# A decode step with cached keys: keys of one group per partition, and V's product from a zeroed tile with four diagonal blocks

## The chip, the core and the metric

The kernel runs on one core of one Trainium2 chip. The metric is the device time in microseconds (us) of one execution; the time of a version is the median over its runs. Engines are named as in the profile: PE (matrix products; PEld its weight loads), DVE (vector), ACT (scalar), POOL, and SP, which only issues DMAs here. The profile is of one execution, and its lines name a line of the kernel as L340.

## The reference

One token `x` (1024 values) goes through attention over a window of cached keys and, beside it, through an MLP; everything is added up.

```python
xn = layernorm(x)                                   # eps 1e-5, no gain
# attention: 32 query heads, 4 key/value heads ("groups"), 128 values a head, the last W = 4096 of 65536 keys
q = (xn @ wq).reshape(1, 1, 32, 128)                # wq 1024 x 4096
k = repeat(k_cache[:, :, -4096:, :], 8, axis=1)     # caches 1 x 4 x 65536 x 128
v = repeat(v_cache[:, :, -4096:, :], 8, axis=1)
p = softmax(q . k * 128 ** -0.5)                    # over the 4096 keys
a = (p . v).reshape(1, 1, 4096) @ wo                # wo 4096 x 1024
# MLP
y = layernorm(xn)
m = gelu_tanh(y @ w1 + b1) @ w2 + b2                # w1 1024 x 3584, w2 3584 x 1024
out = x + a + m
```

All inputs and the output are bfloat16. The weights and the windows of the caches are 39.9 MB, read once.

## The kernel before

**Plan.** The kernel lists its operations in one order by hand (`op`, `dma`), each with the names that it reads and writes. `Plan.emit` gives each engine its own operations in that order and adds a semaphore wait wherever an operation needs a result of another engine or of a DMA. An engine works its list strictly in order. A POOL operation that reads what the POOL operation before it wrote also waits for that one's semaphore.

**Loads.** Nearly all loads are issued by SP on one queue, in this order: one eighth of wq, K (four loads, one per group), the rest of wq (1, 2 and 4 MiB), b1, b2, w1 (two halves), V, w2 (three pieces), wo (two loads of 2 MiB, then five of 2, 1, 0.5, 0.25 and 0.25 MiB). They share four slots of 128 partitions x 32 KB: `slot[0]` holds K, then half of w1, then half of wo; `slot[1]` wq, w1, w2; `slot[2]` wq, V, the other half of wo; `slot[3]` the transposed scratch of K, then w2. A load into a slot waits until the slot's last reader is through; those behind it on SP wait with it.

**K and V in SBUF.** `load_k(g)` puts 32 rows of 32 KB (128 keys each) on the partitions g, g+4, g+8 and so on, so that four neighbouring partitions hold one row of each of the four groups. V is loaded with 32 keys of each group per partition, four pieces of 8 KB.

**Scores.** DVE transposes K in blocks of 32x32 (L340, four operations of 128x4096, into `slot[3]`), and ACT (18 copies, L345) and DVE (10 copies of 32x4096, L349) gather the blocks into `kT`, the keys with the head's 128 values over the partitions. The query goes through wq on PE into `acc2`, is copied to `q_sb` (L394, L395), turned by products with `selq` into `qo_ps`, and written as four blocks of 8 heads into the zeroed `qm` (L422). The score products (recorded at L233, tile `sc_ps`) take 4 column strips of 32 at a time, keys strided: the moving operand runs over (b, u, r) with every fourth key, the output likewise. `sc` is 128 x 1024: partition 32 R + head.

**Softmax.** `sc` is copied from PSUM (L433, L434); the maximum per partition (L441) is turned to a row (L443), joined over the four strips (L445, L447), turned back (L448), and ACT takes the exponential into `e128` with the row sums `l_loc` (L456). DVE transposes `e128` in 32x32 blocks into `eTb` (L460). The sums are joined through `sel4` (L462) to `rs`, one per head, and `grs` is `rs` under the mask `gmask` of a head's own group (L466).

**V's product.** `v_step` (L499 to L501) runs 32 steps, 30 of them in a PE loop of two per turn: weights `eTb[:, 32c : 32c+128]`, of which only the first 32 columns (32 heads) matter, moving operand the V of all four groups, 512 columns. So rows 0-31 of `qo_ps` hold each head against all four groups. DVE multiplies by `grs`, which leaves the own group (L517), adds over the groups (L519) and casts to `o_bf` (L521). Four products with `spread` bring it to 128 partitions (`o8_ps`), which ACT casts to `o8` (L544).

**MLP and the end.** w1's products run on PE in two parts: `w1_part(0)` behind the scores, `w1_part(1)` behind the maxima. `h_pre` (L470, DVE), Gelu (L472, ACT), the transpose `hT` (L474, DVE). Of w2's 28 rows, DVE adds 21 into `run[0]` and `run[1]` (L488 and L485), nine ahead of L517 and twelve behind L521 in its order; PE takes seven after V's product (`bulk_rows(PE_ROWS, ...)` into `sc_ps`), then wo's rows 0-23 into the same banks. L524 joins the two sums, L556 adds `sc_ps` to them, and PE, between wo's rows 27 and 28, adds that sum over the partitions by products with ones (L572, recorded at L239) into `acc2`. L575 (DVE) and L576 (ACT) copy the result, and SP and ACT store half of it each.

**POOL** writes the constants at the start (`spread` L260-261, `ident_f`, `selq`, `gmask` L272-275), computes two powers, zeroes `xw`, `qm`, `b1x` and `run[0]` (L327), and, once b2 has landed, adds x and b2 (L330) and places them in `run[0]` (L331); then it zeroes the last 96 columns of `eTb` (L459).

Of the kernel before, what the change touches and what calls it, by code (L numbers as in the profile page):

```python
# [7 lines left out]
FP32 = mybir.dt.float32  # L8
# [6 lines left out]
class Plan:  # L15
# [11 lines left out]
    def emit(self, done):  # L27
# [53 lines left out]
        ends.append(left)  # L81
        for n in done:
            value[n] = (nc.alloc_semaphore(f"dma{n}"), 16)
        for n, (eng, fn, r, w, dma, _) in enumerate(ops):
            if dma is not None:
                if n in done:
                    continue
                value[n] = (nc.alloc_semaphore(f"dma{n}") if dma is True else dma, 16)
                used.append(value[n][0])
            elif n in wanted:  # L90
                ticks[eng] += 1
                value[n] = (sems[eng], ticks[eng])
# [46 lines left out]
def kernel(  # L139
# [40 lines left out]
    def sb(name, shape, dt):  # L180
        return nc.alloc_sbuf_tensor(name, shape, dt).ap()
# [13 lines left out]
    k_sem = [nc.alloc_semaphore(f"k{g}") for g in range(Hkv)]  # L195
# [3 lines left out]
    def load_k(g):  # L199
        return nc.sync.dma_start(out=k_sb[g:P - Hkv + g + 1:Hkv, :],  # L200
                                 in_=A_k_cache[0, g, Sk - W:Sk, :].rearrange("(r c) d -> r (c d)", r=P // Hkv))
# [12 lines left out]
    def op(eng, fn, r=(), w=()):  # L214
        plan.add(eng, fn, r, w)
# [26 lines left out]
    for g in range(Hkv):  # L242
        plan.add("sp", lambda: None, (), (f"k{g}",), k_sem[g])
# [7 lines left out]
    for i, a, b in wq_cuts:  # L251
# [19 lines left out]
    gmask = sb("gmask", [Hq, Hkv], FP32)  # L271
    op("pool", lambda: pool.memset(gmask, 1.0), (), ("gmask",))  # L272
    op("pool", lambda: pool.affine_select(out=gmask, in_=gmask, compare_op=ALU.is_ge, fill=0.0, base=0,
                                          pattern=[[-REP, Hkv]], channel_multiplier=1), ("gmask",), ("gmask",))
    op("pool", lambda: pool.affine_select(out=gmask, in_=gmask, compare_op=ALU.is_ge, fill=0.0, base=REP - 1,
                                          pattern=[[REP, Hkv]], channel_multiplier=-1), ("gmask",), ("gmask",))

# [5 lines left out]
    for u in range(4):  # L283
# [33 lines left out]
       ("xn", "st12c", "st12g"), ("yT",))  # L317
    sel4 = sb("sel4", [P, Hq], FP32)
    op("dve", lambda: dve.tensor_reduce(out=sel4, in_=ident_f.rearrange("p (r h) -> p h r", r=4), axis=AX.X, op=ALU.add), ("ident_f",), ("sel4",))
    qm = sb("qm", [P, Hkv, Hq], BF16)  # L320
# [11 lines left out]
                                          compare_op=ALU.is_equal, fill=0.0, base=0, pattern=[[-1, Hq], [0, Hq]], channel_multiplier=1), ("xb32",), ("run0",))  # L332

# [5 lines left out]
    for s in range(NS):  # L339
        op("dve", lambda s=s: dve.transpose(out=scr[:, s, :], in_=k2[:, s, :]), ("k0", "k1", "k2", "k3", "slot0"), (f"scr{s}",))  # L340
# [38 lines left out]
    qz, zrow = qm.rearrange("p g h -> p (g h)")[0:Hq, :], spread.rearrange("p u n -> p (u n)")  # L379
# [19 lines left out]
    v4 = v_sb.rearrange("p (g c d) -> p g c d", g=Hkv, c=NCH)  # L399
    dma("sp", v_sb.rearrange("p (g n) -> p g n", g=Hkv), A_v_cache[0, :, Sk - W:Sk, :].rearrange("g (p c) d -> p g (c d)", p=P), (), ("v0",), ("slot2",))  # L400
# [19 lines left out]
    qm_d = qm.rearrange("p g h -> p (g h)")  # L420
    qm_d = bass.AP(tensor=qm_d.tensor, offset=qm_d.offset, ap=[list(qm_d.ap[0]), [Hq + REP, Hkv], [1, REP]])
    op("dve", lambda: dve.tensor_copy(out=qm_d, in_=qT_ps.rearrange("p k g -> p g k")), ("qo",), ("qm",))  # L422
    for g in range(Hkv):
# [34 lines left out]
    eTb = sb("eTb", [P, WQ4 + 96], BF16)  # L458
    op("pool", lambda: pool.memset(eTb[:, WQ4:], 0.0), (), ("eTb_pad",))  # L459
    op("dve", lambda: dve.transpose(out=eTb[:, :WQ4], in_=e128), ("e128",), ("eTb",))  # L460
# [35 lines left out]
    o_all = qo_ps[0:Hq, :]  # L496
    v_in = ("eTb", "eTb_pad", "v0", "slot2")

    def v_step(c, first, last):  # L499
        cols = eTb[:, bass.ds(32 * c, P)] if not isinstance(c, int) else eTb[:, 32 * c:32 * c + P]  # L500
        return pe.matmul(qo_ps, lhsT=cols, rhs=v4[:, :, c, :], start=first, stop=last)  # L501
# [78 lines left out]
    plan.emit([len(plan.ops) - 2, len(plan.ops) - 1])  # L580
# [30 lines left out]
```

## Time and profile before

| | before |
|---|---|
| median of 3 runs (lowest to highest) | 99.91 us (99.87 to 100.18) |
| the profiled execution: its own time | 99.88 us |
| its span from first to last instruction | 98.6 us |
| busy: PE, DVE, ACT, POOL | 59.4, 73.9, 30.8, 10.0 us |
| read from HBM | 39.86 MB, 404 GB/s over the span |
| V's product, start to end | 59.66 to 73.84 us |

The chain of waits is followed back from the last instruction; its pieces in order of time say what each moment of the span waited for. A timeline line gives start and length in us, engine, line, operation, out<-in with shapes, how many, and in brackets the idle time before it and what ended that. Several operations of one kind are merged to one line (x4), whose length then spans them. The rows of w1, w2, wo and the scores on PE all have the helper's line, L233 (weight loads L225, plain products L239), and are told apart by tile and shape.

### The profile page before, as it was taken

What the parts mean: (1) busy time and instruction counts of PE and PEld (TensorE: products, weight loads), DVE (VectorE), ACT (ScalarE), POOL (GpSimd) and SP (SyncE); (2) the same over time, 40 slices, a digit from 0 to 9 for tenths busy, and PEclk for the clock granted to TensorE, in tenths of its full rate; (3) what the DMA queues carried; (4) which work ended last, traced back from release to release, by engine and by line L of the source; (5) the groups of instructions that cost most, each with busy time, mean ns of one, the idle gap of its engine ahead of it and who ended that gap; (6) DMA issues with size and microseconds to landing.
All of it is one profiled execution on the core that took longest, in us unless ns stands there. A gap on an engine that the chain in (4) does not pass through costs nothing.

```text
span 98.6 us, 958 instructions
## 1 busy us (share of the span) xinstructions
PE 59.4 (60%) x323; PEld 16.6 (17%) x220; DVE 73.9 (75%) x75; ACT 30.8 (31%) x29; POOL 10.0 (10%) x22
## 2 busy tenths in 40 slices
PE   0032040599400699940899566887671899995792
PEld 0022000123000234400212111212211111111130
DVE  0023777999999999999103685999999999999231
ACT  0050000089999899992002095000000000000001
POOL 0072580000000670000000000000000000000000
PEclk9999999999998558995559999579998558999999
DMA  2999979999999899899799999999998999999970
GB/s 60 443 442 439 479 316 475 425 525 425 425 425 404 384 407 512 384 407 512 311 425 425 425 437 434 419 425 459 430 489 371 432 425 445 432 425 382 401 288 1
DMA packets 3133, 39.86 MB, mean 404 GB/s; under 512 B 439, under 2 KB 445, under 8 KB 829
## 3 DMA queue, kind: packets, MB, share of 16 engines
q1 hardware_dynamic: 3082, 39.86, 95.5%
q10 hardware_dynamic: 50, 0.00, 0.0%
q14 instruction: 1, 0.00, 0.0%
HBM read 39.86 MB, written 0.00 MB: 404 GB/s over the span
## 4 chain that ended last, share of the span: by engine, by line
DMA 64%; PE 25%; issue 4%; SPq 1%; DVE 0%
DMA slot<-in_A_wq_dram 27%; DMA slot<-in_A_wo_dram 20%; DMA slot<-in_A_v_cache_dram 17%; PE qo_ps L501 11%; PE acc L375 10%; PE acc L233 2%; PE acc L239 1%; SPq L219 1%; DVE res L575 0%
## 5 line engine op out<-in xcount | busy, mean ns | idle before, releaser
L345 ACT COPY kT<-slot 32x1024 bf16<-32x1024 bf16 (+1 forms) x18 | 23.9, 1327 | 14.2 <-DVE slot L340 14.0
L488 DVE SCALAR_TENSOR_TENSOR run<-slot,hTf,run 128x1024 f32<-128x1024 bf16 x20 | 24.2, 1270 | 0.0
L375 PE MATMUL acc<-slot,xw 128*128 x48 | 16.1, 514 | 11.6 <-DMA slot<-in_A_wq_dram 11.6
L340 DVE STREAM_TRANSPOSE slot<-slot 128x4096 bf16<-128x4096 bf16 x4 | 17.4, 4413 | 1.1 <-DMA slot<-in_A_k_cache_dram 1.1
L501 PE MATMUL qo_ps<-slot,eTb 128*128 (+1 forms) x32 | 11.3, 436 | 4.2 <-issue 2.9
L349 DVE COPY kT<-slot 32x4096 bf16<-32x4096 bf16 x10 | 13.2, 1316 | 0.2
L233 PE MATMUL sc_ps<-slot,o 128*1 128x512 bf16 x48 | 9.1, 379 | 1.6 <-DMA slot<-in_A_wo_dram 1.6
L375 PEld LDWEIGHTS acc<-slot,xw 128*128 x48 | 5.7, 118 | 22.7 <-issue 20.2
L576 ACT CAST res<-acc 33x224 bf16<-33x224 f32 x1 | 0.3, 339 | 20.4 <-PE acc L233 20.4
L233 PE MATMUL sc_ps<-slot,hT 128*1 128x512 bf16 x14 | 6.0, 618 | 0.5 <-DMA slot<-in_B_w_dram 0.5
L233 PE MATMUL sc_ps<-kT,qm 128*32 128x512 bf16 x32 | 5.7, 914 | 0.3 <-DVE qm L422 0.3
L501 PEld LDWEIGHTS qo_ps<-slot,eTb 128*128 (+1 forms) x32 | 3.1, 98 | 12.1 <-issue 8.7
L544 ACT CAST o<-misc 128x32 bf16<-128x32 f32 x1 | 0.2, 187 | 14.6 <-PE misc L239 14.6
L434 DVE COPY sc<-sc_ps 128x512 f32<-128x512 f32 x1 | 0.7, 692 | 5.3 <-PE sc_ps L233 5.3
L225 PEld LDWEIGHTS <-o 128*1 128x1 bf16 x40 | 2.4, 85 | 11.6 <-issue 10.9
L239 PE MATMUL misc<-x,spread 32*128 32x8 bf16 x4 | 0.3, 168 | 6.2 <-POOL spread L261 6.2
L239 PE MATMUL acc<-spread,qm 32*128 32x512 bf16 x4 | 1.6, 497 | 3.7 <-POOL qm L321 3.7
L255 DVE MEMSET mhalf<- 128x1 f32 x1 | 0.1, 59 | 5.0 <-PEq L209 5.0
L233 PE MATMUL acc<-slot,yT 128*1 128x448 bf16 x64 | 3.5, 353 | 0.0
L433 ACT COPY sc<-sc_ps 128x512 f32<-128x512 f32 x1 | 0.6, 591 | 8.4 <-PE sc_ps L233 8.4
L239 PE MATMUL qo_ps<-selq,q_sb 128*128 128x4 bf16 x8 | 0.4, 169 | 4.0 <-DVE q_sb L394 4.0
L257 ACT ACT_TABLE_LOAD x1 | 1.3, 1283 | 4.8 <-PEq L209 4.8
(88 smaller groups left out, 48.1 us busy)
## 6 DMA issues: line engine op xcount, KB each, us to landing
slot<-in_B_w_dram SPq DMA_DIRECT2D x3, 3584.0 KB, 16.6
slot<-in_A_wo_dram SPq DMA_DIRECT2D x3, 2048.0 KB, 23.2
slot<-in_A_k_cache_dram SPq DMA_DIRECT2D x4, 1024.0 KB, 9.6
slot<-in_A_wq_dram SPq DMA_DIRECT2D x1, 4096.0 KB, 26.9
slot<-in_A_v_cache_dram SPq DMA_DIRECT2D x1, 4096.0 KB, 16.5
slot<-in_A_wq_dram SPq DMA_DIRECT2D x2, 1024.0 KB, 9.1
slot<-in_A_wq_dram SPq DMA_DIRECT2D x1, 2048.0 KB, 17.7
slot<-in_B_w_dram SPq DMA_DIRECT2D x1, 2048.0 KB, 21.5
```

The source lines that it names most:

```text
L219: plan.add(eng, lambda: q.dma_start(out=out_ap, in_=in_ap), r, w, True, over)
L225: return pe.add_instruction(mybir.InstLdweights(name=nc.get_next_instruction_name(), engine=i.engine, tile_size=(P, 32), tile_position=pos ...
L233: return pe.add_instruction(mybir.InstMatmult(name=nc.get_next_instruction_name(), engine=i.engine, start_tensor_calc=start, stop_tensor_c ...
L239: op("pe", lambda: pe.matmul(out_ap, lhsT=w_ap, rhs=x_ap, start=start, stop=stop, tile_position=pos), r, w)
L257: op("act", lambda: act.activation(out=dummy[:, 0:1], in_=mhalf[0:1, 0:1], func=ACT.Exp), ("mhalf",), ("act_warm",))
L340: op("dve", lambda s=s: dve.transpose(out=scr[:, s, :], in_=k2[:, s, :]), ("k0", "k1", "k2", "k3", "slot0"), (f"scr{s}",))
L345: op("act", lambda s0=s0, s1=s1, R=R, Cd=Cd: act.copy(out=kT[32 * Cd:32 * Cd + 32, R, s0:s1, :].rearrange("p s (c j) -> p (s c) j", j=32), ...
L349: op("dve", lambda R=R, Cd=Cd: dve.tensor_copy(out=kT[32 * Cd:32 * Cd + 32, R, :, :].rearrange("p s (c j) -> p (s c) j", j=32), in_=T3[32 ...
L375: pe.matmul(acc2[:, b, :], lhsT=xw[:, bass.ds(32 * n + 512 * i, P)], rhs=slot[1 + i][:, bass.ds(1024 * n + 512 * b, 512)], start=False, st ...
L434: op("dve", lambda: dve.tensor_copy(out=sc[:, 0:512], in_=sc_ps[:, 0, :]), ("sc0",), ("scs0",))
L488: op("dve", lambda: dve.scalar_tensor_tensor(out=t, in0=wap, scalar=hTf[:, c:c + 1], in1=t, op0=ALU.mult, op1=ALU.add), (key, "hTf", f"run ...
L501: return pe.matmul(qo_ps, lhsT=cols, rhs=v4[:, :, c, :], start=first, stop=last)
```

## The change

- **Loads.** K is one load of 128 rows of 32 KB; partition 32 g + r holds keys 128 r to 128 r + 127 of group g. V is loaded in the same arrangement, 128 pieces of 32 KB instead of 512 of 8 KB.
- **Scores.** `kT[:, g]` now holds the keys of one group, so each of the four column strips works on one group g, and the four products that add up on a strip (u) are for the four blocks of 8 heads: `qm` has for each g and u a 32-column block that is zero outside columns 8u to 8u + 7. Row 32 g + 8 u + h of `sc` is head h of group g for the u-th quarter of the keys in each partition's 128. The moving operand reads runs of 32 neighbouring keys, and the output is written in order. As many weight loads and products as before. The maxima and sums are joined over u instead of over strips (`m_row`, `m_rep`, `sel4`), and `rs` is spread to 128 rows by `selr`.
- **Exponentials.** `eTb` holds after the transpose, for each partition 32 g + r, 128 keys x 8 heads. Four copies of 32 partitions (DVE, ACT, POOL, ACT) put these 8 columns at columns 8 g to 8 g + 7 of each 32-column block of `eM` (128 x 32 x 4 x 32), which POOL has zeroed.
- **V's product.** Step w takes four keys of every partition: weights `eM_w[:, 128 w : 128 w + 128]` (4 keys x 32 heads), moving operand the same four keys' V (4 x 128). Block u of the rows against block u of the columns is wanted: the four diagonal blocks of 32 x 128, which DVE, ACT, ACT and DVE copy into `o_u`, and which the products with `spread_f` (f32, 128 rows) add up while they spread the heads to 128 partitions. The division by the sum moves into ACT's copy to `o8` (`scale=rs`).
- **Gone**: `gmask` and its three POOL operations, `grs`, the zeroed tail of `eTb`, L517, L519, L521.
- **Output.** The two last copies count on one semaphore, so each of the two stores waits once instead of twice.

```diff
+        copied = nc.alloc_semaphore("copied")
+        ends.append(copied)
+        for n in last:
+            value[n] = (copied, len(last))
...
-    k_sem = [nc.alloc_semaphore(f"k{g}") for g in range(Hkv)]
+    k_sem = nc.alloc_semaphore("k")
...
-    def load_k(g):
-        return nc.sync.dma_start(out=k_sb[g:P - Hkv + g + 1:Hkv, :],
-                                 in_=A_k_cache[0, g, Sk - W:Sk, :].rearrange("(r c) d -> r (c d)", r=P // Hkv))
+    k_rows = A_k_cache[0, :, Sk - W:Sk, :].rearrange("g (r c) d -> g r (c d)", r=P // Hkv)
...
-    for i, sem in [(nc.sync.dma_start(out=slot[1][:, 0:NQ], in_=wq_v[:, 0, :]), wq_sem)] + [(load_k(g), k_sem[g]) for g in range(Hkv)] + [(nc.scalar.dma_start(out=x32, in_=x_flat.rearrange("(a j) -> a j", a=Hq)), x_sem)]:
+    for i, sem in [(nc.sync.dma_start(out=slot[1][:, 0:NQ], in_=wq_v[:, 0, :]), wq_sem)] + [(nc.sync.dma_start(out=k_sb, in_=k_rows), k_sem)] + [(nc.scalar.dma_start(out=x32, in_=x_flat.rearrange("(a j) -> a j", a=Hq)), x_sem)]:
...
+    selr = sb("selr", [P, P], FP32)
...
-    op("dve", lambda: dve.tensor_reduce(out=sel4, in_=ident_f.rearrange("p (r h) -> p h r", r=4), axis=AX.X, op=ALU.add), ("ident_f",), ("sel4",))
-    qm = sb("qm", [P, Hkv, Hq], BF16)
+    op("dve", lambda: dve.tensor_reduce(out=sel4.rearrange("p (g h) -> p g h", g=Hkv), in_=ident_f.rearrange("p (g u h) -> p g h u", g=Hkv, u=4),
+                                        axis=AX.X, op=ALU.add), ("ident_f",), ("sel4",))
+    op("dve", lambda: dve.tensor_copy(out=selr.rearrange("p (h q) -> p h q", q=4), in_=sel4.unsqueeze(2).to_broadcast([P, Hq, 4])), ("sel4",), ("selr",))
+    qm = sb("qm", [P, Hkv, 4, Hq], BF16)
...
+    eM = sb("eM", [P, NCH, 4, Hq], BF16)
+    op("pool", lambda: pool.memset(eM, 0.0), (), ("eM",))
+    spread_f = sb("spread_f", [P, 4, P], FP32)
+    op("pool", lambda: pool.memset(spread_f, 0.0), (), ("spread_f",))
+    for u in range(4):
+        op("pool", lambda u=u: pool.affine_select(out=spread_f, in_=spread_f, compare_op=ALU.not_equal, fill=1.0, base=P * u,
+                                                  pattern=[[-1, 4], [1, P]], channel_multiplier=-4), ("spread_f",), ("spread_f",))
...
-    v4 = v_sb.rearrange("p (g c d) -> p g c d", g=Hkv, c=NCH)
-    dma("sp", v_sb.rearrange("p (g n) -> p g n", g=Hkv), A_v_cache[0, :, Sk - W:Sk, :].rearrange("g (p c) d -> p g (c d)", p=P), (), ("v0",), ("slot2",))
+    dma("sp", v_sb, A_v_cache[0, :, Sk - W:Sk, :].rearrange("g (r c) d -> g r (c d)", r=P // Hkv), (), ("v0",), ("slot2",))
...
-    qm_d = qm.rearrange("p g h -> p (g h)")
-    qm_d = bass.AP(tensor=qm_d.tensor, offset=qm_d.offset, ap=[list(qm_d.ap[0]), [Hq + REP, Hkv], [1, REP]])
-    op("dve", lambda: dve.tensor_copy(out=qm_d, in_=qT_ps.rearrange("p k g -> p g k")), ("qo",), ("qm",))
-    for g in range(Hkv):
-        for R in range(4):
-            ldw(qm[:, g, :], (0, 32 * R), ("qm",))
+    qm_d = bass.AP(tensor=qm.tensor, offset=qm.offset, ap=[list(qm.ap[0]), [4 * Hq, Hkv], [Hq + REP, 4], [1, REP]])
+    op("dve", lambda: dve.tensor_copy(out=qm_d, in_=qT_ps.rearrange("p k g -> p g k").unsqueeze(2).to_broadcast([P, Hkv, 4, REP])), ("qo",), ("qm",))
+    for u in range(4):
+        for g in range(Hkv):
+            ldw(qm[:, g, u, :], (0, 32 * g), ("qm",))
...
-            for R in range(4):
-                kv = kT[:, R, :, :].rearrange("p u (b r h) -> p h b u r", r=8, h=Hkv)[:, g, 16 * a:16 * a + 16]
-                mm(sc_ps[32 * R:32 * R + 32, a, :].rearrange("p (b r u) -> p b u r", r=8, u=4), qm[:, g, :], kv,
-                   g == 0, g == Hkv - 1, (0, 32 * R), kt_keys, (f"sc{a}",))
+            for g in range(Hkv):
+                kv = kT[:, g, :, :].rearrange("p s (w u r) -> p u (s w) r", u=4, r=32)[:, u, 16 * a:16 * a + 16, :]
+                mm(sc_ps[32 * g:32 * g + 32, a, :].rearrange("p (w r) -> p w r", r=32), qm[:, g, u, :], kv,
+                   u == 0, u == 3, (0, 32 * g), kt_keys, (f"sc{a}",))
...
-    m_row = sb("m_row", [1, Hq], FP32)
-    op("dve", lambda: dve.tensor_reduce(out=m_row, in_=mT_ps.rearrange("a (r h) -> a h r", r=4), axis=AX.X, op=ALU.max), ("misc",), ("m_row",))
-    m_rep = sb("m_rep", [1, 4, Hq], FP32)
-    op("dve", lambda: dve.tensor_copy(out=m_rep, in_=m_row.unsqueeze(1).to_broadcast([1, 4, Hq])), ("m_row",), ("m_rep",))
+    m_row = sb("m_row", [1, Hkv, REP], FP32)
+    op("dve", lambda: dve.tensor_reduce(out=m_row, in_=mT_ps.rearrange("a (g u h) -> a g h u", g=Hkv, u=4), axis=AX.X, op=ALU.max), ("misc",), ("m_row",))
+    m_rep = sb("m_rep", [1, Hkv, 4, REP], FP32)
+    op("dve", lambda: dve.tensor_copy(out=m_rep, in_=m_row.unsqueeze(2).to_broadcast([1, Hkv, 4, REP])), ("m_row",), ("m_rep",))
...
-    mm32(mc_ps, m_rep.rearrange("a r h -> a (r h)"), ones_f[0:1, 0:1], True, True, ("m_rep", "ones_f"), ("misc",))
+    mm32(mc_ps, m_rep.rearrange("a g u h -> a (g u h)"), ones_f[0:1, 0:1], True, True, ("m_rep", "ones_f"), ("misc",))
...
-    eTb = sb("eTb", [P, WQ4 + 96], BF16)
-    op("pool", lambda: pool.memset(eTb[:, WQ4:], 0.0), (), ("eTb_pad",))
-    op("dve", lambda: dve.transpose(out=eTb[:, :WQ4], in_=e128), ("e128",), ("eTb",))
-    rs_ps = misc[0:Hq, 144:145]
-    mm32(rs_ps, sel4, l_loc, True, True, ("sel4", "l_loc"), ("misc",))
-    rs = sb("rs", [Hq, 1], FP32)
+    eTb = sb("eTb", [P, NCH * 4, REP], BF16)
+    op("dve", lambda: dve.transpose(out=eTb.rearrange("p c h -> p (c h)"), in_=e128), ("e128",), ("eTb",))
+    for g, e in enumerate(("dve", "act", "pool", "act")):
+        q = slice(32 * g, 32 * g + 32)
+        dst = eM[q, :, :, REP * g:REP * g + REP].rearrange("p w u h -> p (w u) h")
+        op(e, lambda e=e, q=q, dst=dst: act.copy(out=dst, in_=eTb[q]) if e == "act" else plan.engines[e].tensor_copy(out=dst, in_=eTb[q]), ("eTb", "eM", "spread_f"), (f"eM{g}",))
+    rs_ps = misc[:, 144:145]
+    mm32(rs_ps, selr, l_loc, True, True, ("selr", "l_loc"), ("misc",))
+    rs = sb("rs", [P, 1], FP32)
...
-    grs = sb("grs", [Hq, Hkv], FP32)
-    op("dve", lambda: dve.tensor_scalar_mul(out=grs, in0=gmask, scalar1=rs), ("gmask", "rs"), ("grs",))
...
-    o_all = qo_ps[0:Hq, :]
-    v_in = ("eTb", "eTb_pad", "v0", "slot2")
-    def v_step(c, first, last):
-        cols = eTb[:, bass.ds(32 * c, P)] if not isinstance(c, int) else eTb[:, 32 * c:32 * c + P]
-        return pe.matmul(qo_ps, lhsT=cols, rhs=v4[:, :, c, :], start=first, stop=last)
+    v_in = ("eM0", "eM1", "eM2", "eM3", "v0", "slot2")
+    eM_w = eM.rearrange("p w u h -> p (w u h)")
+    def v_step(w, first, last):
+        if isinstance(w, int):
+            cols, keys = eM_w[:, P * w:P * w + P], v_sb[:, 512 * w:512 * w + 512]
+        else:
+            cols, keys = eM_w[:, bass.ds(P * w, P)], v_sb[:, bass.ds(512 * w, 512)]
+        return pe.matmul(qo_ps, lhsT=cols, rhs=keys, start=first, stop=last)
...
-    o_m = sb("o_m", [Hq, Hkv, Dh], FP32)
-    op("dve", lambda: dve.tensor_tensor(out=o_m, in0=o_all.rearrange("h (g d) -> h g d", g=Hkv), in1=grs.unsqueeze(2).to_broadcast([Hq, Hkv, Dh]), op=ALU.mult), ("qo", "grs"), ("o_m",))
-    o_f = sb("o_f", [Hq, Dh], FP32)
-    op("dve", lambda: dve.tensor_reduce(out=o_f, in_=o_m.rearrange("h g d -> h d g"), axis=AX.X, op=ALU.add), ("o_m",), ("o_f",))
-    o_bf = sb("o_bf", [Hq, Dh], BF16)
-    op("dve", lambda: dve.tensor_copy(out=o_bf, in_=o_f), ("o_f",), ("o_bf",))
+    o_u = sb("o_u", [P, Dh], FP32)
+    for u, e in enumerate(("dve", "act", "act", "dve")):
+        blk = (slice(32 * u, 32 * u + 32), slice(Dh * u, Dh * u + Dh))
+        op(e, lambda e=e, blk=blk: (act.copy if e == "act" else dve.tensor_copy)(out=o_u[blk[0]], in_=qo_ps[blk]), ("qo",), (f"o_u{u}",))
...
-        mm32(o8_ps, spread[:, q, :], o_bf[:, 32 * q:32 * q + 32], q == 0, q == 3, ("spread", "o_bf"), ("misc",))
+        mm32(o8_ps, spread_f[:, q, :], o_u[:, 32 * q:32 * q + 32], q == 0, q == 3, ("spread_f", "o_u0", "o_u1", "o_u2", "o_u3"), ("misc",))
...
-    op("act", lambda: act.copy(out=o8, in_=o8_ps), ("misc",), ("o8",))
+    op("act", lambda: act.activation(out=o8, in_=o8_ps, func=ACT.Copy, scale=rs), ("misc", "rs"), ("o8",))
...
-    plan.emit([len(plan.ops) - 2, len(plan.ops) - 1])
+    end = len(plan.ops)
+    plan.emit([end - 2, end - 1], [end - 4, end - 3])
```

More of the change, by code (lines that the diff above doesn't have):

```diff
@@ L25, in add, with emit @@
         self.ops.append((eng, fn, tuple(r), tuple(w), dma, tuple(over)))
-    def emit(self, done):
+    def emit(self, done, last):
         nc, ops = self.nc, self.ops
@@ L89, in emit @@
                 used.append(value[n][0])
-            elif n in wanted:
+            elif n in wanted and n not in last:
                 ticks[eng] += 1
@@ L241 @@
     plan.add("sp", lambda: None, (), ("wq0",), wq_sem)
-    for g in range(Hkv):
-        plan.add("sp", lambda: None, (), (f"k{g}",), k_sem[g])
+    plan.add("sp", lambda: None, (), ("k",), k_sem)
     plan.add("act", lambda: None, (), ("x32",), x_sem)
@@ L270 @@
                                           pattern=[[32, 4]], channel_multiplier=1), ("selq",), ("selq",))
[L271 to L276, printed above, removed]
     ones_f = sb("ones_f", [P, P], FP32)
@@ L339 @@
     for s in range(NS):
-        op("dve", lambda s=s: dve.transpose(out=scr[:, s, :], in_=k2[:, s, :]), ("k0", "k1", "k2", "k3", "slot0"), (f"scr{s}",))
+        op("dve", lambda s=s: dve.transpose(out=scr[:, s, :], in_=k2[:, s, :]), ("k", "slot0"), (f"scr{s}",))
     pairs = [(R, Cd) for R in range(4) for Cd in range(4)]
@@ L377, in wq_rows @@
         return rows
-    qz, zrow = qm.rearrange("p g h -> p (g h)")[0:Hq, :], spread.rearrange("p u n -> p (u n)")
+    qz, zrow = qm[0:Hq, 0, :, :].rearrange("p u h -> p (u h)"), spread.rearrange("p u n -> p (u n)")
     for b in range(2):
@@ L419 @@
             mm32(qT_ps[:, k, :], blk, selq, True, True, (f"q_sb{b}", "selq"), ("qo",))
-    qm_d = qm.rearrange("p g h -> p (g h)")
-    qm_d = bass.AP(tensor=qm_d.tensor, offset=qm_d.offset, ap=[list(qm_d.ap[0]), [Hq + REP, Hkv], [1, REP]])
-    op("dve", lambda: dve.tensor_copy(out=qm_d, in_=qT_ps.rearrange("p k g -> p g k")), ("qo",), ("qm",))
-    for g in range(Hkv):
-        for R in range(4):
-            ldw(qm[:, g, :], (0, 32 * R), ("qm",))
+    qm_d = bass.AP(tensor=qm.tensor, offset=qm.offset, ap=[list(qm.ap[0]), [4 * Hq, Hkv], [Hq + REP, 4], [1, REP]])
[3 more added lines that the diff above has]
+            ldw(qm[:, g, u, :], (0, 32 * g), ("qm",))
         for a in range(2):
-            for R in range(4):
-                kv = kT[:, R, :, :].rearrange("p u (b r h) -> p h b u r", r=8, h=Hkv)[:, g, 16 * a:16 * a + 16]
-                mm(sc_ps[32 * R:32 * R + 32, a, :].rearrange("p (b r u) -> p b u r", r=8, u=4), qm[:, g, :], kv,
-                   g == 0, g == Hkv - 1, (0, 32 * R), kt_keys, (f"sc{a}",))
+            for g in range(Hkv):
+                kv = kT[:, g, :, :].rearrange("p s (w u r) -> p u (s w) r", u=4, r=32)[:, u, 16 * a:16 * a + 16, :]
+                mm(sc_ps[32 * g:32 * g + 32, a, :].rearrange("p (w r) -> p w r", r=32), qm[:, g, u, :], kv,
+                   u == 0, u == 3, (0, 32 * g), kt_keys, (f"sc{a}",))
     w1_part(0)
```

## The prediction

> **What bounds the kernel now.** I read the page's DMA rows first, then the chain of waits, then the timeline around each operation that the change touches.
>
> ```profile
> DMA  2999979999999899899799999999998999999970
> q1 hardware_dynamic: 3082, 39.86, 95.5%
> DMA 64%; PE 25%; issue 4%; SPq 1%; DVE 0%
> ```
>
> One queue is busy from the second slice to the last but one, 95.5% of the span: 39.86 MB. Compute is free as long as it never starves that queue and is done when the last rows of wo land. The chain of waits shows what follows them.
>
> ```profile
> 5.62 26.91 DMA slot<-in_A_wq_dram
> ...
> 43.02 16.51 DMA slot<-in_A_v_cache_dram
> ...
> 74.24 19.55 DMA slot<-in_A_wo_dram
> ...
> 93.83 1.03 PE acc L233 x16
> 94.87 0.86 PE acc L239 x8
> 95.73 0.66 PE acc L233 x12
> 96.39 0.02 issue
> 96.41 0.30 PE acc L233 x2
> ```
>
> From 93.8 us on PE is never free: wo rows 24-27, then the sum of `run` and `bulk` (L239), then rows 28-31. L239 needs L556, the last DVE work. So DVE has little room at the end. How much, these timeline rows say:
>
> ```profile
> 47.66 5.69 PE L233 MATMUL sc_ps<-kT,qm 128*32 128x512 bf16 x32 [0.29 <-DVE qm L422]
> 53.09 1.77 PE L233 MATMUL acc<-slot,yT 128*1 128x448 bf16 x32
> 58.14 1.25 DVE L460 STREAM_TRANSPOSE eTb<-e 128x1024 bf16<-128x1024 bf16 x1 [0.20 <-ACT e L456]
> 59.66 1.01 PE L501 MATMUL qo_ps<-slot,eTb 128*128 128x512 bf16 x3 [1.28 <-DMA slot<-in_A_v_cache_dram]
> ...
> 90.22 1.23 DVE L524 TENSOR_TENSOR run<-run 128x1024 f32<-128x1024 f32 x1
> ...
> 91.34 1.89 PE L233 MATMUL sc_ps<-slot,o 128*1 128x512 bf16 x16 [1.27 <-DMA slot<-in_A_wo_dram]
> 93.27 1.28 DVE L556 TENSOR_TENSOR run<-sc_ps,run 33x512 f32<-33x512 f32 x2 [1.82 <-PE sc_ps L233]
> ```
>
> L556 waited 1.82 us for PE, and PE 1.27 us for wo. V's product starts 0.1 us after V lands (59.53), with the exponentials ready at 59.39.
>
> **Loads.** V: 4 MiB landed at 59.53 in 8 KB pieces, the load ahead of it (w1's second half, issued 32.9, 16.6 to landing) at 49.55, so 9.98 us. The 4 MiB of wq in 32 KB pieces landed at 32.53, the load ahead (issued 5.1, 17.7 to landing) at 22.8: 9.73. V in 32 KB pieces therefore gains about 0.25 us. K's pieces are 32 KB before and after: 0. [...] Three of four K issues vanish (4 take 2.45 us), so all engines start some 1.8 us earlier; this gains nothing, as the transposes wait for K (15.45) and the queue is full. One wait fewer before the output: up to 0.05.
>
> **What POOL gets.** gmask's three operations go (0.45 us, early, hidden). New are a memset of `eM` (128x4096), one of `spread_f` (128x512) and four selects on it. They stand behind L331, which waits for b2 landing at 32.7, so they start at 35.2, inside DVE's ten kT copies (32.9 to 46.2). What happens there:
>
> ```profile
> 33.08 2.19 POOL L331 TENSOR_SCALAR_AFFINE_SELECT run<-xb 32x1024 f32<-32x1024 f32 x1
> 35.23 1.24 POOL L459 MEMSET eTb<- 128x96 bf16 x1
> ...
> 34.17 2.19 DVE L349 COPY kT<-slot 32x4096 bf16<-32x4096 bf16 x1
> 36.37 1.22 DVE L349 COPY kT<-slot 32x4096 bf16<-32x4096 bf16 x1
> ...
> 12.59 1.82 DVE L316 TENSOR_SCALAR yT<-xn,st 128x8 bf16<-128x8 f32 x1 [0.67 <-POOL st L314]
> 12.64 0.84 POOL L326 MEMSET b1x<- 128x896 bf16 x1
> 13.43 0.95 POOL L327 MEMSET run<- 128x1024 f32 x1
> ```
>
> These rows exclude each other. L331 stood until the first copy ended (34.15), then worked 1.0 us, and the second copy took 2.19 instead of 1.22. L459's 96 columns took 1.24, until that copy ended. A 128x8 operation (yT) took 1.82 us and ended 0.03 after the memset of `run`. So a POOL memset delays a DVE copy by its own length. Lengths: memsets of 1024 and 128 columns took 0.95 and 0.19, 0.85 ns a column, the same in bf16 (0.84 for 896); 4096 columns make 3.55, 512 make 0.51. The nearest row to the selects is L261, of the same pattern on 32 partitions, 0.64: four are 2.55. Sum 6.6; I take 6.5, since the start of a DVE operation hides about 0.1. kT is then done at 52.7. Bounds: 0, if POOL were held back until DVE is through, and 7.1 (memset at 0.95 for each 1024, selects at 0.7).
>
> **Scores.** qm is written 128 columns wide instead of 32: +0.1 (L422 0.19). The score products now read runs of 32 keys and write in order. They went in fours, eight in turn: 0.85 apart at clock 0.50, 0.46 at full clock. w1's products (448 contiguous columns, full clock) went 0.22 per four (1.77/8). So contiguous costs half: 8 x 0.43 = 3.4 at half clock, which PE has again after its idle stretch, instead of 5.7, less what the full clock gave the last four. I take -2.1; bounds 0 (the layout isn't the cause) and -3.7 (full clock).
>
> **Ahead of V's product.** Four copies of 32x1024 from `eTb` into `eM`. ACT has two, 1.04 each (L345, same shape), behind its table load and warm-up, which end 0.2 after the transpose: 2.3 in all. DVE: 0.35 to 1.1; POOL: 1.0 (L331's work) to 2.2. ACT ends last; PE's first product waits for all four, later by 2.1. Gelu is queued behind them on ACT. Sum: 6.5 + 0.1 - 2.1 + 2.1 = 6.6, so V's product runs from 66.3 to 80.5 (14.2 before: same 32 steps of 128 x 512). That is soon enough for wo's second half, queued behind loads that land until 86.4; past about 83 the queue would run dry.
>
> **Side path.** h_pre follows the eM copy on DVE (65.5), Gelu the ACT copies (67.1), hT 68.8; the first nine w2 rows on DVE run 69 to 79.3 instead of 63.64 to 74, still ahead of V's end.
>
> **After V.** L517, L519 and L521 took 73.85 to 75.77; two copies of 32x128 on DVE (0.2 each, as L521) and two on ACT take 0.5. DVE gains 1.4. Its last twelve rows are queued behind its two copies: 81.0 to 95.4, L524 to 96.6, L556 to 97.9 (94.55 before). The room was 1.82 + 1.4, and 0.2 between L556 and L239: 6.6 - 3.5 = 3.1. PE: the f32 product with `spread_f` costs 0.5 per piece (L239's f32 weights, two loads 0.50), 2.0 instead of 0.28; w2's rows start at 83.1, and with 3.0 at full clock, 7.2 for wo's first 16 rows and 1.9 for the next eight, PE is done at 95.2, ahead of DVE. scale=rs on o8 is free (rs long ready). selr, sel4, m_row, m_rep: under 0.3, hidden or even.
>
> **Sum.** The profiled execution took 99.88 (span 98.6 and 1.28 around it), 0.03 under the median of three, 99.91. 99.88 + 3.1 = **103.0**. V's 0.25 and the wait of 0.05 don't show, since DVE's sum, no longer the landing, ends the kernel.
>
> **Rivals.**
> - *PE at half clock in w2's rows.* Before, the clock was 0.50 from 75.5 to 82.3 and the seven rows took 5.96 instead of 3.0. For: V's end is again followed by weight loads and waits; against: the pause is 0.5 instead of 2 us. PE then ends `bulk` at 98.2, and the end is 4.7 later: 104.6.
> - *Less exclusion.* Only the memset of `eM` holds DVE (3.5): V starts 3.6 late, 0.1 beyond the room, and a slower copy adds some: 100.3. For: selects wait on each other, and could fall into DVE's gaps; against: L331 is such a select, and delayed a copy by all its work.
> - *The loads stay the bound (not slower).* If POOL yields and its work falls between or after DVE's copies, V's product starts at most 0.1 late, under the room of 3.5; below a delay of 3.5 the end is set by wo's landing, earlier by V's 0.25: 99.6. For: POOL did wait for copies one and two. Against: copy two waited as well.
> - *Rows 16 MiB apart.* K's and V's rows of four groups, 16 MiB apart (65536 keys of 256 B), are now read at the same time. If that halved the rate, K alone adds 9.7: 109 or more. Against: wq's rows, 64 KB apart, and V before, whose pieces also come from four groups, went at full rate. [...]
>
> **Numbers.** Chances: forecast 0.45, half clock 0.25, less exclusion 0.13, loads stay the bound 0.13, far rows 0.04. The measurement tells 0.3% (0.3 us) from no change. Slower: 0.45 + 0.25 + 0.04 + most of 0.13 = 0.85; faster and same share the fourth case, at their border: 0.06 and 0.09, with a little of the third. The forecast's own range is 101.6 (scores gain 3.7) to 104.2; the range goes down to the fourth case, 99.6, and up to 105.0 for the half clock.
>
> **What would show it.** In the profile after: kT copies ending near 52.7, one of them over 4 us; score products of some 3.5 us; L501 starting near 66, released by an eM copy rather than V; DVE without a pause before L556, and L239 waiting for it; V landing 9.7 us after the load ahead. If the kT copies end near 46, the forecast is wrong; if PE enters w2's rows at 0.50 and DVE waits at L556, the first rival holds.

## The result and the profile after

The changed kernel took 257.02 us (median of six runs, 254.94 to 260.0) beside 99.89 for the kernel before on the same chip (99.79 to 100.18): a ratio of 2.562, 95% interval 2.553 to 2.570. The forecast was 103.0, its range ended at 105.0. The profiled execution took 260.0, 1.2% above the median: 256.6 of span and 3.4 around it, where before had 98.6 and 1.28. Two of the six runs, the profiled one among them, were in a slower state at 260 and are left out of the ratio; the other four had spans of 251.7 to 254.2, so 2 to 5 us of what follows belong to that state. The sum that has to be explained in the profile is 158.0 us inside the span and 2.1 outside it.

From the page of after, the DMA row of the timeline, the row of the loading queue, the chain by engine, and the group of K's transposes (in a group: busy time, mean ns of one, then idle time before it and what ended it):

```profile
DMA  7999993222222221998299999999982222227910
q1 hardware_dynamic: 2626, 39.86, 62.5%
another core or an unknown queue 62%; DVE 17%; PE 8%; DMA 8%; issue 2%; POOL 1%; ACT 0%; SPq 0%; POOLq 0%; DVEq 0%
L344 DVE STREAM_TRANSPOSE slot<-slot 128x4096 bf16<-128x4096 bf16 x4 | 17.4, 4413 | 79.0 <-DMA slot<-in_A_k_cache_dram 79.0
```

The bytes are the same 39.86 MB, but two long stretches show a DMA share of two tenths. The chain gives 62% of the span to a queue that it can't name; the group's row names it: VectorE stood 79.0 us before the first transpose, for K. The chain of waits, in order of time (start, length, what), shows both places:

```profile
13.28 78.96 another core or an unknown queue
92.26 17.43 DVE slot L344 x4
...
110.97 5.65 DVE kT L353
...
138.18 79.57 another core or an unknown queue
```

K is complete at 92.26 instead of 15.45, V at 217.8 instead of 59.53. From V's landing to the end of the span before took 39.1 us (98.6 - 59.5), and after takes 38.8 (256.6 - 217.8). So the whole loss lies ahead of V's landing: 76.8 in K, and 81.4 between K and V. Everything that the prediction computed for the engines is covered by these two waits, and had to be looked for in other kernels.

Two facts of the trace say what K's load does. A load's semaphore shows an update for each of its landings. K's received four (82.7, 83.2, 91.3 and 92.2 us, after one update at the issue), V's also four (209.5 to 217.8), while in the kernel before each load of K, V and the weights received 16. And a 32 KB piece took about 2.5 us (median) while K was under way, instead of 1.213. K is 128 pieces, over four engines 32 each. They ran from 4.95 to 92.2 us, so 2.7 us each on the engine that ended last: 2.5 or 3.8 while other engines moved wq, until about 41 us, and 2.3 in the mean from 45 to 80. Over sixteen engines at 1.213 it would be 9.7 in all. The loss has two factors, four from the number of engines and a little over two from the duration of a piece.

### The profile page after: what moved, and what is told of

Read it like the earlier page. It is cut to its first block, busy times and chain, and to the rows that moved or that the text cites. A ratio compares the mean times of both kernels' runs of the same rounds, so it can differ in the third digit from the quotient of the medians.

```text
span 256.6 us, 975 instructions
## 1 busy us (share of the span) xinstructions
PE 56.4 (22%) x327; PEld 16.9 (7%) x224; DVE 78.8 (31%) x75; ACT 33.4 (13%) x33; POOL 20.6 (8%) x25
## 3 DMA queue, kind: packets, MB, share of 16 engines
q1 hardware_dynamic: 2626, 39.86, 62.5%
HBM read 39.86 MB, written 0.00 MB: 155 GB/s over the span
## 4 chain that ended last, share of the span: by engine, by line
another core or an unknown queue 62%; DVE 17%; PE 8%; DMA 8%; issue 2%; POOL 1%; ACT 0%; SPq 0%; POOLq 0%; DVEq 0%
DMA slot<-in_A_wo_dram 8%; DVE kT L353 7%; DVE slot L344 7%; PE qo_ps L506 4%; PE acc L235 1%; PE sc_ps L235 1%; PE misc L241 1%; DVE yT L310 1%; DVE m_loc L443 0%; DVE xn L299 0%; PE acc L241 0%; DVE q_sb L398 0%; POOL spread L262 0%; ACT sc L435 0%
## 5 line engine op out<-in xcount | busy, mean ns | idle before, releaser
L506 PE MATMUL qo_ps<-slot,eM 128*128 (+1 forms) x32 | 11.1, 436 | 82.8 <-DMA slot<-in_A_v_cache_dram 79.7
L353 DVE COPY kT<-slot 32x4096 bf16<-32x4096 bf16 x10 | 18.3, 1831 | 0.2
L379 PEld LDWEIGHTS acc<-slot,xw 128*128 x48 | 5.6, 116 | 101.4 <-issue 99.0
L506 PEld LDWEIGHTS qo_ps<-slot,eM 128*128 (+1 forms) x32 | 3.1, 98 | 90.5 <-issue 88.5
L327 POOL TENSOR_TENSOR xb<-x,b 32x32 f32<-32x32 bf16 x1 | 0.2, 233 | 96.7 <-DMA b<-in_B_b_dram 96.7
L335 POOL TENSOR_SCALAR_AFFINE_SELECT spread_f<-spread_f 128x512 f32<-128x512 f32 x4 | 5.7, 1427 | 0.6
L235 PE MATMUL sc_ps<-slot,hT 128*1 128x512 bf16 x14 | 4.9, 524 | 0.9 <-DMA slot<-in_B_w_dram 0.9
L331 POOL MEMSET eM<- 128x4096 bf16 x1 | 3.5, 3501 | 0.0
L235 PE MATMUL sc_ps<-kT,qm 128*32 128x512 bf16 x32 | 3.3, 586 | 0.4 <-DVE qm L424 0.4
L465 POOL COPY eM<-eTb 32x1024 bf16<-32x1024 bf16 x1 | 1.3, 1282 | 15.7 <-DVE eTb L461 15.7
L235 PE MATMUL acc<-slot,o 128*1 128x288 bf16 (+1 forms) x32 | 2.2, 272 | 0.6 <-DMA slot<-in_A_wo_dram 0.6
L310 DVE TENSOR_SCALAR yT<-xn,st 128x8 bf16<-128x8 f32 x1 | 2.1, 2136 | 0.7 <-POOL st L308 0.7
```

Source lines behind the costliest of these rows:

```text
L235: return pe.add_instruction(mybir.InstMatmult(name=nc.get_next_instruction_name(), engine=i.engine, start_tensor_calc=start, stop_tensor_c ...
L310: op("dve", lambda: dve.tensor_scalar(out=yT, in0=xn, scalar1=st12[:, 2:3], scalar2=st12[:, 6:7], op0=ALU.subtract, op1=ALU.mult), ("xn", ...
L331: op("pool", lambda: pool.memset(eM, 0.0), (), ("eM",))
L335: op("pool", lambda u=u: pool.affine_select(out=spread_f, in_=spread_f, compare_op=ALU.not_equal, fill=1.0, base=P * u, pattern=[[-1, 4], ...
L353: op("dve", lambda R=R, Cd=Cd: dve.tensor_copy(out=kT[32 * Cd:32 * Cd + 32, R, :, :].rearrange("p s (c j) -> p (s c) j", j=32), in_=T3[32 ...
L379: pe.matmul(acc2[:, b, :], lhsT=xw[:, bass.ds(32 * n + 512 * i, P)], rhs=slot[1 + i][:, bass.ds(1024 * n + 512 * b, 512)], start=False, st ...
```

## Experiments on the loads

The table view by windows gives both factors at once: the window and its length, busy time (and instructions) of PE, PEld, DVE, ACT and POOL, granted clock, DMA share and GB/s. A share of 0.25 is four of sixteen engines, as K's four landings. Before, in the stretch in which K loads:

```profile
6.00:15.00 9.00, 2.47 (x10) 1.31 (x10) 4.91 (x17) 0.24 (x2) 5.14 (x14) 1.00 0.99 425
```

After, while K alone loads:

```profile
45.00:80.00 35.00, 0.00 (x0) 0.00 (x0) 0.00 (x0) 0.00 (x0) 0.00 (x0) 1.00 0.25 56
```

Per busy engine that is 425 / (0.99 x 16) = 27 GB/s before and 56 / (0.25 x 16) = 14 after. What differs is the access pattern: K's source in one load runs over [4 groups, 32 rows, 4096], groups 16 MiB apart, while each of the four loads before ran over 32 rows. The landings fit the outermost dimension of the source in the loads here: 4 gives four, 128 and 32 give sixteen, and loads of 16 rows (below) kept all engines busy (a DMA share of 0.97). Even the trace of before has a case of four: b1's load, four rows, landed four times (32.2 to 32.3). Which rule deals the pieces to engines beyond these cases is not shown.

The half rate was the open question. The theories were the distance of the rows in memory (rival 4) and the partitions that the engines write. The code below is cut from longer lines ("..."), and in the versions with several loads each operation that uses K or V waits for all of them.

**Four loads each, same arrangement.** Groups stay on 32 neighbouring partitions (V in the same way):

```
-... (nc.sync.dma_start(out=k_sb, in_=k_rows), k_sem) ...
+... (nc.sync.dma_start(out=k_sb[32 * g:32 * g + 32, :], in_=k_rows[g]), k_sem[g]) for g in range(Hkv) ...
```

> The changed kernel with K and V loaded in four loads each, one per group (32 rows of 32 KB onto 32 neighbouring partitions); all else as changed. Theory A (a load whose outermost dimension is the 4 groups is carried by 4 of the 16 DMA engines; everything else behaves about as forecast): each load again counts on 16 engines, K lands near 15.5 us, and the time is 101.3, worked out with the sizes that the changed kernel's own trace shows (kT copies 5.1 longer, scores 2.4 shorter). Rival B (the arrangement itself, one group on 32 neighbouring partitions, loads slowly however it is split): over 150. If nothing of the compute matters: 99.6.

Measured: 122.93 (122.57 to 123.17), ratio 1.230 (1.228 to 1.232). Sixteen landings a load, yet 1 MiB came every 4.9 to 5.0 us (landings 11.1, 16.2, 21.2, 26.1) instead of 2.43, a piece at 2.55 (median). The window over K's load:

```profile
7.00:26.00 19.00, 1.62 (x4) 0.63 (x4) 4.93 (x15) 0.00 (x0) 4.24 (x6) 1.00 0.96 203
```

All engines busy, half the bytes: 203 / (0.96 x 16) = 13 GB/s per engine. The four engines were most of the loss (257 to 123), but the arrangement itself halves the rate, although at any time all engines read one group, so no rows 16 MiB apart.

**K alone in one load** (V as in the experiment above).

> V in four loads as in e1_four_loads, K in one load as in the change. This prices K's load alone. Theory A: half of the loss, 170 to 185; K's semaphore gets 4 landings from DMA engines, K's 32 KB pieces take some 2.5 us as in the changed kernel (1.21 before), and the last lands 80 to 92 us after the start. Rival B: the same as e1_four_loads.

Measured: 203.3 (one run), above the 170 to 185 expected; the last of four landings at 92.2, pieces of 2.44 us (median) and 55 GB/s in the window from 45 to 80 us. So one load instead of four costs 80 us for K (203.3 - 122.9), and for V, on top of K's, about another 54 (257.0 - 203.3).

**K in one load, its four blocks near each other.** The blocks come from one group, 33 rows (1.03 MiB) apart instead of 16 MiB (V in four loads):

```
+k_all = A_k_cache[0, 0, 0:132 * 128, :].rearrange("(b r c) d -> b r (c d)", b=4, c=128)
+k_rows = k_all[:, 0:32, :]
```

> As e2_k_one_load, but K's four blocks of 1 MiB are read from 1.03 MiB (33 rows of 32 KB) apart inside one group instead of 16 MiB apart; so the scores are of other keys. Still 4 DMA engines. Theory HBM (the pieces take twice as long because four engines read 16 MiB apart): 32 KB pieces at 1.21 us, K there by about 45 us, time 125 to 140. Theory port (they take twice as long because of where the four engines write): pieces at 2.5 as before, 170 to 185.

Measured: 203.48 (one run), pieces of 2.41 (median), 58 GB/s in the same window. The distance changes nothing here, so it isn't what halves the rate. It could still have cost something that the other limit hides; the next experiment answers that.

**Still four engines, still 16 MiB apart, but other partitions.** Each of four loads takes eight rows of every group onto 32 neighbouring partitions, so the four engines write partitions 8 apart instead of 32 (V in four loads):

```
+... (nc.sync.dma_start(out=k_sb[32 * g:32 * g + 32, :], in_=k_rows[:, 8 * g:8 * g + 8, :]), k_sem[g]) for g in range(Hkv) ...
```

> As e2_k_one_load, but K in four loads, each of 8 rows from each of the four groups onto 32 neighbouring partitions; still 4 DMA engines and still 16 MiB apart, but the four engines now write partitions 8 apart instead of 32 apart. Keys stand on other partitions than the kernel takes them for. Theory port: 32 KB pieces at 1.21 us, K there by about 45 us, time 125 to 140. Theory HBM: pieces at 2.5, 170 to 185.

Measured: 169.71 (one run). Four landings a load, the last of them at 23.3, 42.6, 52.2 and 61.9. While the other engines still loaded, pieces took 2.3 to 2.55, so K was complete at 61.9 and not near the 45 expected; from 42 us on, with four engines alone, 1.213:

```profile
42.00:60.00 18.00, 0.00 (x0) 0.00 (x0) 0.00 (x0) 0.00 (x0) 0.00 (x0) 1.00 0.24 106
```

The same share of 0.24, at 106 instead of 56 GB/s, 28 per engine. Number of engines and distance of the groups are as in the change, only the partitions differ: the doubling comes from where the engines write, and with rows 16 MiB apart four engines reach the full rate, so rival 4's mechanism falls. Side by side, per busy engine: 14 GB/s with four engines 32 partitions apart (after), 13 with sixteen engines on 32 neighbouring partitions (four loads), 28 with four engines 8 apart, and 27 with sixteen engines on every fourth partition (before). Why some sets of partitions take half the rate is not shown.

**Can the arrangement be loaded at full rate?** My guess was that it could, if partitions 0 to 63 (groups 0 and 1) and 64 to 127 (groups 2 and 3) were written at the same time. At the rate of before K would then be complete near 15.5 us, at that of the four loads near 26. Three tries. Eight loads of 16 rows, groups in turn 0, 2, 0, 2, 1, 3, 1, 3:

```
+turns = [(g + d, h) for g in (0, 1) for h in (0, 1) for d in (0, 2)]
+... (nc.sync.dma_start(out=k_sb[32 * g + h:32 * g + 31 + h:2, :], in_=k_rows[g][h:32:2]), k_sem[i]) for i, (g, h) in enumerate(turns) ...
```

> The changed kernel with K and V in eight loads each: 16 rows of one group onto every second of its 32 partitions, the loads alternating between the groups of partitions 0-63 and those of 64-127 (0, 2, 0, 2, 1, 3, 1, 3); each load on 16 engines, one 32 KB piece each. [...]

Measured: 119.47 (ratio 1.195, 1.192 to 1.198), 0.5 MiB every 2.35 to 2.4 us, K landed at 25.0: still half rate, with 221 GB/s at a DMA share of 0.97 from 7 to 25 us, 14 per engine. The loads landed one behind the other, so the two halves of the partitions were not written at the same time; why is not shown. The same with POOL's new work put early:

> As e5_alternate_ports, with POOL's constants early as in e7_full_rate_pool_early. If the alternating loads run at full rate, this is the changed kernel without both of its costs: 99.6, 0.3 under the kernel before. If not: 121 to 123.

Measured: 119.67 (1.197, 1.194 to 1.199). And groups 0 and 1 on SP's queue, 2 and 3 on ACT's, with POOL's work early too:

```
+... ((nc.sync if g < 2 else nc.scalar).dma_start(out=k_sb[32 * g:32 * g + 32, :], in_=k_rows[g]), k_sem[g]) for g in (0, 2, 1, 3)
```

> The changed kernel's own arrangement with K and V in four loads each, groups 0 and 1 (partitions 0-63) issued by SP, groups 2 and 3 (partitions 64-127) by ACT, so that both halves of the partitions are loaded at the same time; POOL's constants early. [...] If every DMA engine still works one piece at a time and all stay in step: 119 to 123.

Measured: 121.58 (1.209, 1.198 to 1.220), K landed at 25.4. The loads of the two queues landed in pairs (15.6 and 15.9, 25.2 and 25.4), so both were under way at once, and pieces still took 2.36. Two queues didn't raise the rate either; why not stays open. No way of loading the change's own arrangement at full rate was found, and no version of it beat the kernel before.

## Experiments on the rest of the change

**All of the change, with loads at full rate.** K and V go in four loads onto every fourth partition, as K did before, and every instruction of the change behind the loads runs. It computes on keys of mixed groups, so it prices the change and is no version to use; the same holds for the kernels below that start from it:

```
-... (nc.sync.dma_start(out=k_sb, in_=k_rows), k_sem) ...
+... (nc.sync.dma_start(out=k_sb[g:P - Hkv + g + 1:Hkv, :], in_=k_rows[g]), k_sem[g]) for g in range(Hkv) ...
```

> The changed kernel with K and V loaded in four loads each onto every fourth partition, as K was before. The rows then stand on other partitions than the kernel takes them for, so scores and V's product mix groups; all instructions are those of the change. This prices the change without its loads. Forecast on record 103.0. With the sizes of the changed kernel's trace (kT copies 5.1 longer instead of 6.5, scores 2.4 shorter, eM copies 2.3): V's product starts 5.0 late, 1.5 beyond DVE's room of 3.5: 101.4. Rival, the loads stay the bound: 99.6. V's four loads should land within 9.7 us of the load ahead instead of 10.0.

Measured: 103.65 (103.43 to 103.87), ratio 1.036 (1.034 to 1.039); the profiled execution 103.76, of it 100.4 span. Against the first experiment only the partitions of K and V differ: K was complete at 15.4 instead of 26.1, pieces at 1.213 instead of 2.55. So the partitions decided the rate with sixteen engines as with four. This kernel comes nearest to the one that the prediction priced, and its timeline (start, length, what, idle time before and its releaser) can be held against the forecast:

```profile
32.90 18.44 DVE L354 COPY kT<-slot 32x4096 bf16<-32x4096 bf16 x10
35.23 3.50 POOL L332 MEMSET eM<- 128x4096 bf16 x1
40.42 6.14 POOL L336 TENSOR_SCALAR_AFFINE_SELECT spread_f<-spread_f 128x512 f32<-128x512 f32 x4
52.88 3.59 PE L235 MATMUL sc_ps<-kT,qm 128*32 128x512 bf16 x32 [0.39 <-DVE qm L427]
62.74 2.10 ACT L468 COPY eM<-eTb 32x1024 bf16<-32x1024 bf16 x2
64.89 0.95 PE L509 MATMUL qo_ps<-slot,eM 128*128 128x512 bf16 x3 [3.23 <-ACT eM L468]
95.42 1.28 DVE L562 TENSOR_TENSOR run<-sc_ps,run 33x512 f32<-33x512 f32 x2
96.16 1.24 PE L241 MATMUL acc<-run,ones_f 128*1 128x288 f32 x6 [1.19 <-DVE run L562]
```

The copies end at 51.34, V's product starts at 64.89 released by an `eM` copy, VectorE reaches the last addition (L562) without a pause, and PE waits 1.19 for it. V's own landing was 59.2, 9.7 after the load ahead. The time is 2.3 above the 101.4 expected of this kernel; 2 of these lie outside the span (below).

**POOL's new work earlier.** The memset of `eM`, and `spread_f`, are put ahead of the two operations that wait for b2:

> As e6_full_rate (rows on other partitions than taken for), but POOL zeroes eM and builds spread_f ahead of the operations that wait for b2, so before DVE's kT copies. If POOL's work delays those copies and this sets the end: kT copies end near 46.2 again, V's product starts near 59.6, and the time is 99.6, bound by the loads. If the room of 3.5 was never used up: no difference from e6_full_rate.

Measured: 101.77 (1.018, 1.016 to 1.020), span 98.3, 2.1 under the kernel above and 0.3 under before. The copies now take 12.31 in all. But POOL's work holds VectorE earlier instead. From the timeline:

```profile
12.59 6.05 DVE L311 TENSOR_SCALAR yT<-xn,st 128x8 bf16<-128x8 f32 x1 [0.67 <-POOL st L309]
14.64 3.51 POOL L329 MEMSET eM<- 128x4096 bf16 x1
```

yT took 6.05 instead of 1.82, the transposes start at 18.86 instead of 15.48, and V's product at 62.82, 3.2 after its start before: inside the room of 3.5 that the prediction read, so that the end is the loads' again. From the chain:

```profile
77.30 16.25 DMA slot<-in_A_wo_dram
```

**Eight loads onto every eighth partition**, all else as in the last kernel, meant to show whether the number of instructions decides the time outside the span (next experiment):

```
+... (nc.sync.dma_start(out=k_sb[g + 4 * h:P - 7 + g + 4 * h:8, :], in_=k_rows[g][h:32:2]), k_sem[2 * g + h]) for g in range(Hkv) for h in range(2) ...
```

> As e7_full_rate_pool_early, but K and V in eight loads each of 16 rows, onto every eighth partition; so SP has 8 DMAs more. e8_alternate_pool_early has as many loads and 1.4 outside its span. If the 2 us outside the span hang on how many instructions an engine has: 99.6 to 100.0 with 1.4 outside. If on the change's other parts: 101.8. [...]

Measured: 119.74 (1.194, 1.185 to 1.204), K at 25.5: half rate (210 GB/s at a DMA share of 0.95 from 7 to 25 us, 14 per engine), which I had not expected. On every fourth partition K was complete at 15.4; why every eighth takes half the rate is not shown.

**Two microseconds outside the span.** The kernel with POOL early has a shorter span than before (98.3 against 98.6) and a longer time: 3.2 to 3.6 us lie outside, where before has 1.2 to 1.7 (2.6 in one run). Four edits of it: the two separate output waits restored; eight instructions that do nothing on SP; two on PE; two on VectorE.

> As e7_full_rate_pool_early (rows on other partitions than taken for), but the two last copies count on their engines' semaphores again, so each store waits twice, as before the change. e7's profiled run took 101.77 for a span of 98.3: 3.5 outside the span, where the kernel before has 1.3, and its trace has a 16 KB instruction transfer at the end that the trace of before lacks. If the shared semaphore (one instruction fewer on SP and ACT) brings that about: 99.7. If not: 101.8.

> As e7_full_rate_pool_early (rows on other partitions than taken for), with eight operations that do nothing on SP ahead of w1's loads. Versions with eight loads of K and V each had 1.3 to 1.5 us outside their span, those with four or one had 3.2 to 3.7. If the length of SP's program decides that: 99.7. If not (other engines' programs, or where they lie): 101.7.

> As e7_full_rate_pool_early (rows on other partitions than taken for), with two operations that do nothing on PE ahead of the query's products. The versions without the extra 2 us outside the span had two PE instructions more (438 against 436). If the length of PE's program decides: 99.7. If not: 101.7.

> As e7_full_rate_pool_early, with two operations that do nothing on DVE ahead of its copy of the query. The versions without the extra 2 us outside the span had two DVE instructions more (95 against 93). If the length of DVE's program decides: 99.7. If not: 101.7.

Measured: 101.46, 101.58, 101.77 and 101.59, with 3.1 to 3.6 outside the span in all of them. None of the four edits takes it away. The trace with the two waits has one instruction more on SP and on ACT, as intended; the traces of the other three list no instruction more on SP, PE and VectorE, so that these operations were executed is not shown. What goes with the extra time is a transfer that before doesn't have, here as the page of after lists it (packets, MB, share):

```profile
q8 instruction: 1, 0.02, 0.0%
```

It is 16 KB. In the traces with 2.5 us or more outside the span, one such transfer starts within the last 0.7 us of the span or behind it: at 97.7 of 98.3 with POOL early, at 256.05 of 256.6 in after. In the two kernels with 1.25 to 1.54 outside in every run (eight loads, POOL early) it comes in the middle, at 65.4 and 65.8. The alternating loads without POOL early have both: in the profiled run, 2.5 outside, one transfer at 74.9 and one at 119.8, behind the span; their other four runs had 1.25 to 1.43. That is an association. What this transfer serves, and whether it is what takes the 2 us, stays open.

## Why the prediction was wrong

**The step that failed is "Loads".** It said "K's pieces are 32 KB before and after: 0" and gave V a gain of 0.25. It took the price of a load from the size of its pieces alone, and left out how the pieces are dealt to engines and onto which partitions these write. K's term was 0 and measured 76.8; V's was -0.25 and its share of the span 81.4. The landings per load (16, and 4 for b1's four rows) and the every-fourth placing of K stood in the trace and the code of before; neither was asked for the new pattern, whose outermost dimension is 4. The 9.98 and 9.73 that were compared were both of loads with 16 engines.

**Rival 4 had the place and not the mechanism.** Half rate for K and V was in it, as a bare supposition with a chance of 0.04, from rows 16 MiB apart; no run shows that distance to be what halves the rate. Blocks 1.03 MiB apart gave the same 203 us, and blocks 16 MiB apart went at full rate on other partitions. The range, up to 105.0, had left out the 109 that this rival itself gave. The "against" that I set beside it, that wq and the old V ran at full rate, was true of loads with sixteen landings onto all 128 partitions (9.73 and 9.98 us for 4 MiB), and said nothing of these.

**The rest, by the full-rate kernel.** Direction and bound were right: V's product late, the room gone, VectorE's sum last. Term by term:

- kT copies later by 5.1 (51.34 against 46.2), forecast 6.5. The memset took 3.50 (forecast 3.55) and held a copy by that much. The four selects and the small memset, put at 3.05, cost the remaining 1.6. They excluded the copies as well: each select took 1.43 instead of 0.64 and ended 0.50 after the end of the copy that it met (41.35 and 41.85, 42.92 and 43.42, and so on), and the copy behind it took 1.56 instead of 1.22. So the rule read from L331 held, and the mis-sized term is the price of a select: 0.33 to a copy, not its whole 0.64. The rival "less exclusion" put V's product 3.6 late, too little by 1.6, and its cause, that only the memset holds the copies, was not the case.
- Scores: -2.1, forecast -2.1 (3.59 against 5.69).
- Ahead of V's product: the `eM` copies ran from 62.53 to 64.84, 2.3, forecast 2.1. V's product started 5.2 late (64.89 - 59.66), forecast 6.6; the difference is the selects and the small memset.
- The f32 product took 1.19 for its four pieces, forecast 2.0. The first rival's clock came: 0.50 from 80.8 to 83.7, and the seven rows of w2 took 4.68 instead of 3.0. Its consequence did not, as L562 did not wait for PE. With POOL early, the clock there was 1.00.
- VectorE's last addition ended at 96.7, forecast 97.9; the span rose by 1.8, forecast 3.1.
- V's gain of 0.25 is real (9.7 against 9.98) and, as said, did not show.
- Outside the span: 2.0, in no term. So that 103.65 lies near the forecast of 103.0 is luck: a term too large and one that was missing, not a sum that was right.

With POOL early, which is another order than the prediction's, the loads were the bound again, as in the rival of that name (span 98.3), and still the time was 1.8% above before, by the term outside the span.

## What to carry to other kernels

Before two loads are merged, write down the outermost dimension that is left in the source, and the set of partitions that are written at one moment. Here the number of engines went with the first (4 or 16 landings), the rate of each with the second (14 or 27 GB/s). Four loads whose patterns split into 16 cost 2.45 us of issue; one that split into 4 cost 77 us (K at 92.26 instead of 15.45). In the profile the sign is a DMA share that sits at a fraction such as 0.25 while everything waits, and GB/s divided by the busy engines tells whether each of them is slow as well (here 14 instead of 27).

## What the runs showed of the hardware that I had not expected

- A load on four engines slowed the loads of the others: 16 KB pieces of wq took 1.2 to 1.3 us from 10 to 24 us, beside K's load, and 0.61 from 84 us on. It was slowed by them too: with partitions 8 apart, K's pieces took 2.3 to 2.55 until the other loads were done and 1.213 after, when its four engines, alone, moved 28 GB/s each. Why is not shown.
- Neither alternating the halves of the partitions in one queue nor two queues brought two half-rate loads to full rate together (K at 25.0 and 25.4, against 26.1 plain and 15.4 at full rate).
- POOL's memset and selects took turns with VectorE's copies. A memset of 3.50 us, begun during a copy, held that copy for its whole length (5.65 us in place of 2.19). A select that met a running copy waited for its end (1.43 us instead of 0.64) and cost the next copy 0.33.
